# A decode kernel with interleaved layers: query blocks by columns, wider up products, split transposes, output-projection products by shape, and a new planned order

## The chip, the cores and the metric

The kernel runs on one core of a Trainium2 chip. The metric is the device time of one execution in microseconds (us); three runs of the kernel before gave 268.49, 271.14 and 273.38 us, median 271.14. "Faster" or "slower" means by more than 2%.

The core has a matrix engine (PE in the profile, with its weight loads as a row of their own, PEld), a vector engine (DVE), a scalar engine (ACT), a general engine (POOL) and a sync engine (SP), which here issues almost all DMAs. Each engine runs its own list of instructions in order, and they wait for each other through semaphores.

## The reference

Eight rows (batch 8, one query token each, width 448) go through two identical layers of attention over a cached window followed by a small MLP. Both layers use the same weights and, what matters most here, the same K and V.

```
def _A_ref(x, k_cache, v_cache, wq, wo):      # Hq=16, Hkv=8, Dh=256, W=1024 of Sk=4096 kept
    q = (x @ wq).reshape(B, 1, 16, 256)
    k, v = k_cache[:, :, Sk-W:, :], v_cache[:, :, Sk-W:, :]   # each head pair shares one k/v head
    p = softmax(q @ k^T * 256**-0.5)
    return (p @ v).reshape(B, 1, 16*256) @ wo
def _B_ref(x, w1, w2):                         # 448 -> 1792 -> 448
    return silu(x @ w1) @ w2
x = x + _A_ref(_layernorm(x), ...)
x = x + _B_ref(_layernorm(x), ...)
x = x + _A_ref(_layernorm(x), ...)             # the same K, V, wq, wo again
x = x + _B_ref(_layernorm(x), ...)
```

K and V of one row are 16 tiles of 512 KB (8 heads each of K and V, 1024 positions by 256), 128 tiles in all; with the weights the kernel moves 78.31 MB.

## The kernel before

**Staging.** A K or V tile lands in one of 30 slots (`slots`, `load_kv`, L540). The loads stand in a fixed sequence: K of row 0, V of row 0, K of row 1 and so on, with w2 and wo behind the K of row 0 and w1 behind its V. A load waits until the tile that held its slot 30 places earlier has been used for the last time, and that is its use in the second layer. So the K slots of row b come free after the second layer's scores (four after each half, `attend2`), its V slots after the second layer's value products (four after each half, `pv_rows2`, L788).

**Interleaving.** While row b goes through its first MLP and its second attention, row b+1 goes through its first attention, so that every K and V tile is read once from memory and used twice. One turn of this loop ("a row" below) issues some 510 matmuls. In the planned order before it runs like this: `chain(b)` computes the first layer's residual of row b, its statistics (L847, ACT L850, POOL L852), the up products (L587, L592, L598), tanh, the down products (L871), the residual again, the second layer's queries (L882, ACT L887, turned by L890) and stores them as query blocks (L895, eight stores of 32 partitions by 64 numbers); `scores` (L706) is used three times in it, for the next row's first layer in two halves and for this row's second layer in two halves; `softmax` and `pv_rows1`, `pv_cols1` (L756, L770) finish the first layer of row b+1; `wo_rows` (L810) and `wo_cols` (L825, L828) give its output projection, and `pv_rows2` (L788) the second layer's values of row b.

**Shapes on PE.** Scores, value rows, the wide projections and the query products use 32-column tiles of the array, four of them side by side with outputs at partitions 0, 32, 64 and 96. The up products, `pv_cols1`, `wo_cols` and the folds (L571, L574) load full 128-column weights and stream few columns: 28, 32, 16 and 1. The rest of the 448 columns over 3 x 128 gives products of 64 columns (L598, the second L825 form).

**Query blocks.** For each half k2, `qbd` holds 32 blocks of 8 columns beside each other, one block for each of (head j, column block cb, parity par); a block is the weight of one score matmul. Block `a` of 8 columns is loaded as it lies. The second layer's stores L895 write one of every four columns: 64 numbers, each four places from the last.

**Transposes.** A K tile is transposed in place by two DVE instructions (L690), one for each half of the slot. Both write the key `("slot", s)`, so the second waits for the first through DVE's own semaphore.

**The order.** All engine work is recorded as tasks with an estimated duration, the keys that it reads and writes, and a name. A list scheduler (`schedule`) sorts the tasks of each engine by the length of the chain behind them plus a constant out of the table `BIAS`, with `HOLD` deciding how long it holds an engine for a more urgent task. `emit` then writes each engine's list and the waits that the keys ask for. DMAs keep the order of the program. The durations and `BIAS` do nothing on the chip but set this order.

Of the kernel before, what the change touches and what calls it, by code (L numbers as in the profile page):

```python
# [4 lines left out]
BF16 = mybir.dt.bfloat16  # L5
# [14 lines left out]
HOLD = 0.292  # L20
BIAS = {"act.exp0@0": -2.8, "act.exp0@7": -4.3, "act.exp1": 5.0, "act.exp1@0": -4.6, "act.exp1@7": -14.5,
        "act.exp2": 22.7, "act.exp2@0": -145.4, "act.exp2@7": -65.4, "act.init": 4.9, "act.oev0": 15.9,
        "act.oev0@0": 248.8, "act.oev0@7": -0.4, "act.oev1": -97.9, "act.oev1@0": -26.9, "act.oev1@7": 0.1,
        "act.q1s": -9.2, "act.qrow0": 277.6, "act.qrow0@0": 7.0, "act.qrow0@7": -27.8, "act.qrow1": 22.2,
        "act.qrow1@0": -8.1, "act.qrow1@7": -8.4, "act.rowb1": -4.2, "act.rowb1@0": 4.0, "act.rowb1@7": -218.4,
        "act.rowb2": -22.2, "act.rowb2@0": 77.5, "act.rowb2@7": -0.4, "act.rowb8": 12.4, "act.rowb9": 8.5,
        "act.rowbL@7": 75.1, "act.rsum2@0": 50.6, "act.rsum@0": -13.9, "act.tanh": 19.0, "act.tanh8": 171.0,
        "act.tanh@0": 0.7, "act.tanh@7": 20.5, "act.tanhL@7": -81.0, "act.var1": -8.1, "act.var1@0": -10.1,
        "act.var1@7": 63.5, "act.var2": 6.4, "act.var2@0": -0.6, "act.var2@7": 176.2, "act.varL@7": 1.2,
        "act.x2b@7": -13.1, "act.xr@7": 13.6, "act.zL@7": 70.5, "dve.KT0": 88.4, "dve.KT0@0": 228.9,  # L30
        "dve.KT0@7": 27.9, "dve.KT1": 4.3, "dve.KT1@0": 2.0, "dve.KT2": -26.1, "dve.KT2@0": 15.0, "dve.KT3": -88.4,
        "dve.KT3@0": -4.3, "dve.KT3@7": -44.0, "dve.KT4@7": 5.2, "dve.KT5": -900.3, "dve.KT5@0": -16.4,
        "dve.KT5@7": -221.1, "dve.KT6": -10.5, "dve.KT6@0": 4.0, "dve.KT6@7": -151.6, "dve.KT7@7": -27.1,
        "dve.f8a": 1.8, "dve.h8": -3.2, "dve.hT": -24.0, "dve.hTL@7": -48.7, "dve.init": 1.3, "dve.lsum0": 20.2,
        "dve.lsum0@0": -7.1, "dve.lsum1": 3.6, "dve.lsum1@0": 126.7, "dve.lsum1@7": 118.3, "dve.lsum2@0": -1.6,
        "dve.lsum2@7": 18.9, "dve.mT0": -4.0, "dve.mT0@0": 2.9, "dve.mT0@7": 2.7, "dve.mT1@7": 147.6,
        "dve.mT2": 38.0, "dve.mT2@0": -26.3, "dve.mT2@7": -11.8, "dve.max0": -10.8, "dve.max0@0": 37.1,
        "dve.max0@7": 23.9, "dve.max1": -42.3, "dve.max1@0": -12.3, "dve.max1@7": -1.5, "dve.max2": -29.0,
        "dve.max2@0": -2.9, "dve.max2@7": -32.2, "dve.mb0": -84.7, "dve.mb0@0": -0.8, "dve.mb0@7": -81.8,
        "dve.mb1@0": -5.7, "dve.mb1@7": 9.8, "dve.mb2": 2.2, "dve.mb2@0": 20.0, "dve.mg0": -1.5, "dve.mg0@0": 103.5,  # L40
        "dve.mg1": 29.2, "dve.mg1@7": 1.6, "dve.mg2": -0.5, "dve.mg2@0": 17.1, "dve.mg2@7": 3.4, "dve.oTc4": -102.9,
        "dve.oTc4@0": -7.5, "dve.oTc4@7": -1.9, "dve.oTc5@7": -3.1, "dve.oTc6": 0.9, "dve.oTc6@0": -11.3,
        "dve.oTc6@7": 97.4, "dve.oTc7": 1.3, "dve.oTc7@0": -10.2, "dve.oTc7@7": 15.9, "dve.oTev0": -13.1,
        "dve.oTev0@0": 11.1, "dve.oTev0@7": 57.2, "dve.oTev1@7": -0.8, "dve.orow8": 126.6, "dve.orowL@7": 1.9,
        "dve.q1T": 61.4, "dve.q1r": 3.6, "dve.q1s": -17.2, "dve.qbd2.0": 2.2, "dve.qbd2.0@0": -2.6,
        "dve.qbd2.0@7": -63.5, "dve.qbd2.1": -68.8, "dve.qbd2.1@7": -100.3, "dve.rl0": -39.9, "dve.rl0@7": -123.5,
        "dve.rl1@0": 47.5, "dve.rl2": -88.3, "dve.rl2@7": -5.7, "dve.rsum@0": -13.4, "dve.sqh8": 51.5,
        "dve.turn0": -4.9, "dve.turn0@0": 53.7, "dve.turn0@7": 71.5, "dve.turn1": 132.4, "dve.turn1@7": 41.5,
        "dve.turn2": -2.1, "dve.turn2@7": 30.0, "dve.x0": -16.6, "dve.xb0": 29.6, "dve.xb1": 18.8, "dve.xb1@0": 15.5,
        "dve.xb1@7": -1.8, "dve.xb2": 2.7, "dve.xb2@7": -0.7, "dve.xbL@7": -4.6, "dve.xc8": 1.5, "dve.z8": 0.4,  # L50
        "pe.PV0": -1.9, "pe.PV0@0": 54.1, "pe.PV0@7": -368.9, "pe.PV1.0": -461.7, "pe.PV1.0@0": -856.1,
        "pe.PV1.0@7": -57.7, "pe.PV1.1": -22.9, "pe.PV1.1@0": -151.4, "pe.PVc4": 0.3, "pe.PVc4@0": -3.7,
        "pe.PVc4@7": -21.0, "pe.PVc5": -227.6, "pe.PVc5@0": 85.5, "pe.PVc5@7": 6.7, "pe.PVc6": -0.4,
        "pe.PVc6@7": 45.5, "pe.PVc7@0": -3.6, "pe.PVc7@7": -40.3, "pe.S0.0": -28.8, "pe.S0.1": 301.7,
        "pe.S0.1@0": -140.3, "pe.S1.0": -38.9, "pe.S1.0@0": -25.6, "pe.S1.1": 451.9, "pe.S1.1@0": 225.6,
        "pe.S1.1@7": -4.0, "pe.fold1": -35.5, "pe.fold1@0": 4.2, "pe.fold1@7": -1.1, "pe.fold2": 101.9,
        "pe.fold2@7": 7.5, "pe.fold8": 3.7, "pe.fold9": -13.9, "pe.foldL@7": -32.9, "pe.l0": 3.5, "pe.l0@0": -35.3,
        "pe.l0@7": -4.1, "pe.l1": 34.4, "pe.l1@0": 111.0, "pe.l1@7": 0.9, "pe.l2@7": 87.4, "pe.oT0@0": -3.6,
        "pe.oT0@7": -45.7, "pe.oT1": -3.1, "pe.oT1@0": -3.8, "pe.oT1@7": -4.9, "pe.perm0": 1.5, "pe.perm0@0": -9.7,
        "pe.perm0@7": -55.5, "pe.perm1@0": -113.7, "pe.perm1@7": -6.9, "pe.perm2": -21.4, "pe.perm2@0": 17.2,  # L60
        "pe.perm2@7": -17.1, "pe.q1": -6.3, "pe.q1sel": 42.3, "pe.qd0@7": -9.0, "pe.qd1": 110.5, "pe.qd1@0": -0.4,
        "pe.qd1@7": 0.9, "pe.stat1@0": 91.6, "pe.stat1@7": 110.2, "pe.stat2": 4.1, "pe.stat2@0": -17.8,
        "pe.stat2@7": -22.5, "pe.stat8": 0.3, "pe.statL@7": 9.3, "pe.w18": -84.7, "pe.w1@0": -19.9, "pe.w1@7": 3.9,
        "pe.w2": -3.5, "pe.w28": 98.6, "pe.w2@0": 3.8, "pe.w2L@7": -80.2, "pe.wo": -295.7, "pe.wo4": 47.6,
        "pe.wo4@0": -13.7, "pe.wo4@7": 40.3, "pe.wo5@0": 103.1, "pe.wo6": 5.9, "pe.wo6@0": -137.4, "pe.wo6@7": 107.3,
        "pe.wo8": -26.1, "pe.wo@0": 2.1, "pe.wo@7": 1.8, "pe.woL@7": 9.0, "pe.woc@7": 2.5, "pe.wq0": 187.0,
        "pe.wq0@0": 44.9, "pe.wq0@7": 34.9, "pe.wq1": -9.0, "pe.wq1@0": -8.4, "pe.wq1@7": -2.0, "pe.xT": -1.4,
        "pe.xinit": -11.2, "pe.xinit8": 10.3, "pe.xinit@0": 38.4, "pe.xinit@7": -78.5, "pe.xres8": -80.5,
        "pool.init": -0.6, "pool.pow1": -99.7, "pool.pow1@0": -2.2, "pool.pow1@7": 12.4, "pool.pow2@0": -394.4,
        "pool.pow2@7": 21.8, "pool.pow8": 137.9, "pool.powL@7": -1.1, "pool.qbd1": -58.2, "pool.qbd1@0": -181.8,  # L70
        "sp.out": 1.6, "sp.out8": 1.4, "sp.slot0": 5.3, "sp.slot1": 1.6, "sp.slot10": 0.2, "sp.slot11": -3.7,
        "sp.slot12": -0.2, "sp.slot13": -2.2, "sp.slot14": -2.1, "sp.slot15": -2.1, "sp.slot16": -0.1,
        "sp.slot17": -1.0, "sp.slot18": 2.6, "sp.slot19": -4.0, "sp.slot2": -0.5, "sp.slot20": 5.6, "sp.slot21": 0.1,
        "sp.slot22": 3.6, "sp.slot23": 3.4, "sp.slot24": 3.9, "sp.slot25": 2.2, "sp.slot26": -4.1, "sp.slot27": -0.8,
        "sp.slot28": -1.1, "sp.slot29": -4.6, "sp.slot3": -1.4, "sp.slot4": -3.8, "sp.slot5": -5.0, "sp.slot6": 0.6,
        "sp.slot7": -0.1, "sp.slot8": -2.1, "sp.slot9": -2.9, "sp.w1": -1.6, "sp.w1t0": -1.2, "sp.w1t1": -1.2,
        "sp.w2": -0.2, "sp.wo": -1.3, "sp.wq0": 1.2, "sp.wq1": 1.6, "sp.wq2": 1.1, "sp.wqt0": -2.0, "sp.wqt1": -1.8,
        "sp.x": 1.3}
# [230 lines left out]
def bass_interleave_layers__sliding_block_cached__dense_activation_silu__decode_kernel(  # L309
# [23 lines left out]
    C_W1, CW = 96, 28  # L333
# [6 lines left out]
    sb = nc.alloc_sbuf_tensor  # L340
    wq_sb = sb("wq_sb", [P, 3 * HD + HD2], BF16)
    wo_sb = sb("wo_sb", [P, H * PW], BF16)
    w1_sb = sb("w1_sb", [P, 3 * F + F2], BF16)
    w2_sb = sb("w2_sb", [P, FC // 2 * PW], BF16)
    slots = [sb(f"slot{i}", [P, 2048], BF16) for i in range(R)]
    ident = sb("ident", [P, P], BF16)
    perm = sb("perm", [P, P], BF16)
    qbd = [sb(f"qbd{i}", [P, 520], BF16) for i in range(2)]
    ep = [sb(f"ep{i}", [P, 512], BF16) for i in range(2)]
    q1s = sb("q1s", [P, NB, P], BF16)  # L350
    mm = [sb(f"mm{i}", [P, 32], F32) for i in range(2)]
    mg = [sb(f"mg{i}", [P, 8], F32) for i in range(2)]
# [96 lines left out]
    for i in SC:  # L449
        const(bank[i][:], -1e30, bk(i), dur=0.6)  # L450
# [676 lines left out]
```

## Time and profile before

| what | value |
|---|---|
| median of three runs | 271.14 us (268.49 to 273.38) |
| the profiled execution | 271.07 us, span 268.9 us, granted PE clock 0.922 |
| PE, PEld busy | 197.4 us (73%), 130.6 us (49%), 4547 matmuls and as many loads |
| DVE, ACT, POOL busy | 185.3 us (69%), 58.7 us (22%), 23.0 us (9%) |
| DMA | 78.31 MB, mean 291 GB/s |
| L690 transposes | 128, 86.2 us of DVE, 696 ns each |
| L895 query-block stores | 64, 22.5 us of DVE, 352 ns each |
| L706 scores | 1024, 39.8 us of PE |
| L587, L592, L598 up products with 28 columns | 378, 108 and 36 |
| L825, L828 output projection by columns | 160 and 32 |

The span runs from the first to the last instruction of the program; the execution has 2.2 us around it. Matmuls are pipelined, so the times of many add up to more than they take; where it matters, the distance between the starts is used. A busy share is a mean over phases with different limits. The rows "idle before, releaser" tell how long an engine sat idle in front of a group of instructions and what ended that. "issue" means that the engine waited for nothing that the profile records.

### The profile page before, as it was taken

The page shows a single profiled execution, that of the slowest core. Times are in us where ns is not written, and L with a number is a line of the kernel's source. Part 1 is how long each engine was busy: PE and PEld are TensorE (multiplying, and loading weights), DVE is VectorE, ACT ScalarE, POOL GpSimd, SP SyncE. Part 2 cuts the span into 40 slices and gives each one's busy share as a digit, 9 for nine tenths or more (in the row PEclk, how much of TensorE's full clock was granted, in tenths as well). Part 3 has the DMA queues.
Part 4 walks back from the last instruction along what each step waited for, and adds up shares of the span by engine and source line. Part 5 has one row for each costly group of instructions (what it writes and reads, how often), then busy time and mean ns, then how long its engine had stood idle before and what let it go on. Part 6 is the DMA issues. An engine that isn't in the chain of part 4 may idle for free.

```text
span 268.9 us, 10096 instructions
## 1 busy us (share of the span) xinstructions
PE 197.4 (73%) x4547; PEld 130.6 (49%) x4547; DVE 185.3 (69%) x527; ACT 58.7 (22%) x151; POOL 23.0 (9%) x41
## 2 busy tenths in 40 slices
PE   1051333588799788987898879789978897998885
PEld 1051111353567465645565555457455645654644
DVE  6669969767877786688579766986797479313510
ACT  2000537011220320132022102211222032123121
POOL 1200100000010000000000000001001000000200
PEclk9999999999997999599979986998999689979986
DMA  7999999999498999698979969898999697000000
GB/s 194 414 411 390 381 394 410 419 408 406 178 336 306 381 373 388 249 378 268 380 233 396 389 251 333 327 366 309 340 366 376 243 357 278 10 2 2 2 3 0
DMA packets 22639, 78.31 MB, mean 291 GB/s; under 512 B 2231, under 2 KB 5318, under 8 KB 22214
## 3 DMA queue, kind: packets, MB, share of 16 engines
q1 hardware_dynamic: 22438, 77.31, 76.2%
q8 instruction: 35, 0.57, 0.8%
q10 hardware_dynamic: 160, 0.38, 0.6%
q14 instruction: 6, 0.05, 0.0%
HBM read 77.67 MB, written 0.01 MB: 289 GB/s over the span
## 4 chain that ended last, share of the span: by engine, by line
PE 55%; DVE 18%; DMA 10%; issue 5%; ACT 5%; SPq 4%; POOL 1%; DVEq 0%
DMA wo_sb<-in_A_wo_dram 10%; PE bank L788 9%; DVE qbd L895 8%; PE bank L706 8%; PE bank L810 5%; PE bank L587 5%; DVE slot L519 4%; PE bank L770 4%; PE bank L871 4%; PE bank L882 3%; PE bank L825 3%; PE bank L756 3%; ACT ep L835 2%; SPq L540 2%; PE bank L571 2%
## 5 line engine op out<-in xcount | busy, mean ns | idle before, releaser
L690 DVE STREAM_TRANSPOSE slot<-slot 128x512 uint32<-128x512 uint32 x128 | 86.2, 696 | 9.3 <-DMA slot<-in_A_k_cache_dram 8.1
L706 PE MATMUL bank<-slot,qbd 128*8 128x256 bf16 (+1 forms) x1024 | 39.8, 288 | 18.1 <-DVE qbd L895 12.1
L706 PEld LDWEIGHTS bank<-slot,qbd 128*8 128x8 bf16 (+1 forms) x1024 | 22.1, 87 | 29.1 <-DVE qbd L895 18.4
L895 DVE TENSOR_SCALAR qbd<-bank,fcols 32x64 bf16<-32x64 f32 x64 | 22.5, 352 | 7.8 <-PE bank L890 4.2
L788 PE MATMUL bank<-slot,ep 128*2 128x256 bf16 (+1 forms) x512 | 26.4, 359 | 0.0
L729 ACT ACTIVATE ep<-bank,mm 128x256 bf16<-128x256 f32 x24 | 11.4, 473 | 37.5 <-DVE mm L726 24.0
L770 PE MATMUL bank<-qbd,slot 128*128 128x32 bf16 x512 | 17.2, 178 | 3.1 <-DVE q1s L748 2.4
L852 POOL TENSOR_TENSOR fcols<-fcols 128x1 f32<-128x1 f32 x17 | 9.4, 552 | 116.1 <-ACT fcols L850 116.1
L678 POOL TENSOR_TENSOR qbd<-q1s,fcols 128x256 bf16<-128x256 bf16 x16 | 9.8, 612 | 108.2 <-DVE mg L724 37.2
L770 PEld LDWEIGHTS bank<-qbd,slot 128*128 128x128 bf16 x512 | 15.2, 97 | 7.2 <-issue 4.7
L882 PE MATMUL bank<-wq_sb,q1s 128*1 128x512 bf16 x256 | 17.8, 392 | 0.3 <-DVE q1s L840 0.3
L587 PE MATMUL bank<-q1s,w_sb 128*128 128x28 bf16 x378 | 17.9, 184 | 0.0
L840 DVE SCALAR_TENSOR_TENSOR q1s<-bank,fcols 128x5 bf16<-128x5 f32 x17 | 3.9, 230 | 19.2 <-PE bank L828 14.4
L810 PE MATMUL bank<-wo_sb,q1s 128*1 128x449 bf16 x256 | 15.0, 378 | 2.5 <-DVE q1s L775 2.2
L587 PEld LDWEIGHTS bank<-q1s,w_sb 128*128 128x128 bf16 x378 | 14.8, 102 | 2.7 <-DVE slot L690 1.3
L825 PE MATMUL bank<-q1s,wo_sb 128*128 128x16 bf16 (+1 forms) x160 | 11.4, 183 | 6.0 <-issue 6.0
L788 PEld LDWEIGHTS bank<-slot,ep 128*2 128x2 bf16 (+1 forms) x512 | 13.0, 103 | 5.6 <-issue 0.5
L887 ACT ACTIVATE ep<-bank 128x512 bf16<-128x512 f32 x16 | 9.5, 596 | 19.6 <-PE bank L882 18.2
L756 PE MATMUL bank<-slot,qbd 128*2 128x256 bf16 x256 | 9.2, 290 | 6.0 <-DMA slot<-in_A_v_cache_dram 6.0
L592 PE MATMUL bank<-q1s,w_sb 128*128 128x28 bf16 x108 | 13.2, 183 | 0.0
L825 PEld LDWEIGHTS bank<-q1s,wo_sb 128*128 128x128 bf16 (+1 forms) x160 | 8.8, 103 | 7.4 <-issue 6.6
L850 ACT ACTIVATE fcols<-bank,fcols 128x1 f32<-128x1 f32 x17 | 4.4, 259 | 36.0 <-PE bank L847 35.9
(146 smaller groups left out, 281.4 us busy)
## 6 DMA issues: line engine op xcount, KB each, us to landing
slot<-in_A_k_cache_dram SPq DMA_DIRECT2D x64, 512.0 KB, 8.1
slot<-in_A_v_cache_dram SPq DMA_DIRECT2D x64, 512.0 KB, 7.9
wo_sb<-in_A_wo_dram SPq DMA_DIRECT2D x1, 3584.0 KB, 27.3
wq_sb<-in_A_wq_dram SPq DMA_DIRECT2D x3, 1024.0 KB, 8.9
w_sb<-in_B_w_dram SPq DMA_DIRECT2D x1, 1568.0 KB, 19.6
w_sb<-in_B_w_dram SPq DMA_DIRECT2D x1, 1344.0 KB, 17.3
wq_sb<-in_A_wq_dram ACTq DMA_DIRECT2D x1, 256.0 KB, 3.8
wq_sb<-in_A_wq_dram SPq DMA_DIRECT2D x1, 256.0 KB, 4.4
```

What stands on the lines that cost most here:

```text
L587: fns.append(lambda e, f=f, g=g, s=s, c=c, c0=c0: e.matmul(bank[bank_i][:, c0:c0 + cw], w1_sb[:, c * F + 256 * g + s:c * F + 256 * g + s + ...
L592: fns.append(lambda e, t0=t0, c0=c0, g=g: e.matmul(bank[bank_i][:, c0:c0 + cw], w1_sb[:, t0:t0 + 255:2], rhs(3 + (g > 3)), start=False, st ...
L690: dve(lambda e, v=v: e.transpose(v, v), [("slot", s)], [("slot", s)], 0.15 + n / 2 / 950, b, "KT%d" % k)
L706: fns.append(lambda e, w=w, j=j, kv=kv, cb=cb, par=par: e.matmul(sc[32 * j:32 * j + up_to, c0:c0 + 256], w, kv, start=(cb == 0 and par == ...
L729: act(lambda e: e.activation(e_sb[s], x, ACTF.Exp, bias=m[:, 0:1], scale=1.0), bk(sc) + [("mm", L)], E_KEY[s], 0.47, b, "exp%d" % s)
L756: fns = [lambda e, u=u, j=j: e.matmul(bank[OB[0]][32 * j:32 * j + 2, 0:DH], pT_sb[0][:, 32 * u + 10 + 2 * j:32 * u + 12 + 2 * j], slots[sl ...
L770: fns = [lambda e, a=a, u=u: e.matmul(bank[vb][:, c0 + 32 * a:c0 + 32 * a + 32], v[:, u * DH + a:(u + 1) * DH:2], view(pT_sb[1], 32 * u + ...
L788: fns.append(lambda e, u=u, j=j, w=w, k2=k2: e.matmul(bank[OB[1]][32 * j:32 * j + (4, 2)[k2], 0:DH], w, slots[slot_of[b, "v", 4 * k2 + j]] ...
L810: fns.append(lambda e, i=i, w=w, c0=c0: e.matmul(bank[XB][32 * (i % 4):32 * (i % 4) + 1, c0:c0 + D + 1], oT(i), w, start=(i < 4), stop=(i ...
L825: fns.append(lambda e, c=c, rhs=rhs, row=row: e.matmul(bank[YB][xpart(c), XS * c:XS * (c + 1)], xpiece(row, c), rhs.broadcast_to([P, XS]), ...
L882: pe([lambda e, j=j, c=c, wb=wb, k2=k2: e.matmul(bank[wb][32 * j:32 * j + 1, :], xbt[b][:, xcol(c, k2):xcol(c, k2) + 1], wq_sb[:, c * HD + ...
L895: dve(lambda e, qs=qs, k2=k2, q=q: e.tensor_scalar(view(qbd[1][32 * q:32 * q + 32, :], 8 + 256 * k2 + q, [(4, 64)]), qs, rhalf[0:32, :], 2 ...
```

## The change

**Query blocks by columns.** In each half of `qbd` the 8 columns of a block now lie 32 apart: column n of the block index runs fastest. A score matmul loads its 8 (or 16) weight columns with a step of 32. The second layer's stores write two runs of 32 neighbouring numbers in place of 64 scattered ones. The blocks lose their 8 columns of padding; for the second layer's first half, which loads 16 columns, the 8 columns in front are columns of the identity and the permutation matrix, and their results are overwritten by the second half. The queries of the first layer are stored to match (`q_blocks1`, L678).

**Up products.** Each streams 64 columns (the same column repeated) in place of 28, and the 14 results lie 64 apart across two banks that are now one tensor `pair`. Their first matmul starts the bank afresh, so bank XB is written too, and the products now wait for whatever read XB and YB last. The statistics of both kinds sit in YB.

**Value products by columns** stream 64 or 48 columns in place of 32.

**Transposes.** The two halves write keys of their own, so the second no longer waits for the first; `scores` reads all three keys.

**wo column products.** For the last head the 24 products go by shape: 12 of 128 columns, 4 of the mean with 128, 4 of the first 64-column piece, 4 of the second, in place of 3 + 2 + 1 for each of four chunks.

**Order.** All durations and the tables `BIAS` and `HOLD` are new, and with them the order of the tasks on all engines but SP's. In the steady part PE runs the next row's second score half (32 matmuls) before the second layer's first half where it was behind it, turns the second half's queries and does the value rows (L755 in the new numbering) before the second layer's second half, and splits that half around the first value product by columns; the folds of the residual stand behind a score half; 24 of the 32 first value products of the second layer stand behind the wo column products.

```diff
-    C_W1, CW = 96, 28
+    X0, C_ST, CW = 400, 500, 64
...
-    qbd = [sb(f"qbd{i}", [P, 520], BF16) for i in range(2)]
+    cst = sb("cst", [P, 2 * P + 512], BF16)
+    ident, perm = cst[:, 0:P], cst[:, P:2 * P]
+    qbd = [sb("qbd", [P, 512], BF16)[:, :], cst[:, 2 * P:]]
...
+    pair = nc.alloc_psum_tensor("bank6", [P, 1024], F32)[:, :]
+    bank += [pair[:, 0:512], pair[:, 512:1024]]
...
                 for c in range(3):
-                    fns.append(lambda e, f=f, g=g, s=s, c=c, c0=c0: e.matmul(
-                        bank[bank_i][:, c0:c0 + cw], w1_sb[:, c * F + 256 * g + s:c * F + 256 * g + s + 255:2], rhs(c),
-                        start=False, stop=False, skip_group_check=True))
+                    fns.append(lambda e, f=f, g=g, s=s, c=c, out=out: e.matmul(
+                        out, w1_sb[:, c * F + 256 * g + s:c * F + 256 * g + s + 255:2], rhs(c),
+                        start=(f == 0 and c == 0), stop=False, skip_group_check=True))
...
-            dve(lambda e, v=v: e.transpose(v, v), [("slot", s)], [("slot", s)], 0.15 + n / 2 / 950, b, "KT%d" % k)
+            dve(lambda e, v=v: e.transpose(v, v), [("slot", s)], [("kt", s, h)], 0.065 + n / 2 / 950, b, "KT%d" % k)
...
-                    a = 16 + 256 * k2 + (j * 8 + cb * 2 + par) * 8
-                    w = q[:, a - up_to:a]
+                    a = 256 * (k2 if layer else 1 - k2) + j * 8 + cb * 2 + par
+                    w = (cst[:, a:a + 481:32] if up_to == 16 else qbd[layer][:, a:a + 225:32])
...
-        c0 = (256 + 64 * (j // 2), 160)[j % 2]
+        c0, n = ((256, 64), (160, 48), (384, 64), (160, 48))[j]
...
+        for c in list(range(3)) + [XC] + list(range(3, XC)):
+            for i in range(4 * kvh, 4 * kvh + 4):
+                c0 = i // 2 * PW + R0 + i % 2 * D
+                m0 = i // 2 * PW + (M0, M1)[i % 2]
+                w = wo_sb[:, m0:m0 + 1].broadcast_to([P, P]) if c == XC else xpiece(wo_sb[:, c0:c0 + D], c)
+                part, pos = (slice(0, P), (0, 0)) if c == XC else (xpart(c), xpos(c))
...
-        sbk, col = (YB, 490) if name == "2" else (XB, 480)
-        s2 = bank[sbk][:, col:col + 1]
+        s2 = bank[YB][:, C_ST + (name == "2"):C_ST + (name == "2") + 1]
...
-        w1_cols(YB, C_W1, CW, lambda c: xbt[b][:, c:c + 1].broadcast_to([P, CW]), b, [("xbt", b)], "w1", GROUPS)
+        w1_cols(pair, CW, lambda c: xbt[b][:, c:c + 1].broadcast_to([P, CW]), b, [("xbt", b)], bk(XB) + bk(YB), "w1", GROUPS)
...
                 dve(lambda e, qs=qs, k2=k2, q=q: e.tensor_scalar(
-                    view(qbd[1][32 * q:32 * q + 32, :], 8 + 256 * k2 + q, [(4, 64)]), qs, rhalf[0:32, :], 2.0 * SCALE,
-                    op0=ALU.mult, op1=ALU.mult), bk(lb) + ["rhalf"], [("qbd", 1, k2, q)], 0.13, b,
+                    view(qbd[1][32 * q:32 * q + 32, :], 256 * k2 + 32 * q, [(128, 2), (1, 32)]),
+                    qs.rearrange("p (r n) -> p r n", r=2), rhalf[0:32, :], 2.0 * SCALE,
+                    op0=ALU.mult, op1=ALU.mult), bk(lb) + ["rhalf"], [("qbd", 1, k2, q)], 0.14, b,
                     "qbd2.%d" % k2)
```

Left out are the same layout in `q1sel` and in the turn of the second layer's queries (L890), the new column offsets of bank YB, and the tables of the planner.

## The prediction

> **What bounds the kernel now.** I read the page first: the PE clock by slices, the DMA row, and the groups with the longest idle time before them.
>
> ```profile
> PEclk9999999999997999599979986998999689979986
> DMA  7999999999498999698979969898999697000000
> q8 instruction: 35, 0.57, 0.8%
> ...
> L895 DVE TENSOR_SCALAR qbd<-bank,fcols 32x64 bf16<-32x64 f32 x64 | 22.5, 352 | 7.8 <-PE bank L890 4.2
> ```
>
> The reader is to see that the DMA row is full until 62 us (the tenth slice) and has holes once a row afterwards, and that the clock dips at a steady distance. Up to 62 us the weights set the time: wo lands at 39.2 us, four reductions of 2.9 us on DVE follow. After that no engine is full, so the order of time decides. Next, the chain of waits between 112 and 165 us:
>
> ```profile
> 118.47 0.35 DVE qbd L895
> ...
> 119.62 0.36 DVE qbd L895
> 119.98 0.04 issue
> 120.03 1.11 PE bank L706 x26
> ...
> 132.08 1.20 issue
> ...
> 136.77 1.74 PE bank L788 x32
> 138.52 0.78 PE bank L871 x7
> ```
>
> PE stands still for four stores in a row, and again for the four at 121.57; it stands still for 1.2 us inside the wo column products with nothing recorded that it waits for; and 32 matmuls of L788 take 1.74 us. The starts of L871 on this chain (61.01, 87.42, 112.78, 138.52, 164.50, 189.45, 215.37, 239.48 us) give seven rows in 178.5 us, **25.5 us a row**. The view by stages, cut where the clock changes, explains the slow L788:
>
> ```profile
> 131.49:134.91 3.42, 2.22 (x54) 1.73 (x54) 1.35 (x3) 0.00 (x0) 0.00 (x0) 1.00 0.77 307
> 134.91:138.32 3.41, 3.41 (x85) 2.67 (x85) 3.04 (x7) 0.53 (x2) 0.55 (x1) 0.50 0.62 179
> 155.39:158.80 3.41, 1.86 (x42) 1.35 (x38) 1.75 (x4) 0.20 (x1) 0.61 (x1) 1.00 0.92 366
> 158.80:162.21 3.41, 3.41 (x77) 2.60 (x76) 2.62 (x5) 0.26 (x1) 0.55 (x1) 0.50 0.29 74
> ```
>
> The clock (seventh number) changes on a grid of 3.41 us, and each fall to 0.50 follows a stretch with the stall and the narrow products in it; it lasts one or two steps.
>
> **Part by part, for a row.**
>
> *Clock.* I weigh each matmul by its streamed columns, a quarter for 32-column tiles, a half for 64. The groups of PE in 131.49:134.91 (14 x 16, 8 x 16/2, 16 x 256/4 and 16 x 28) give 1,760, and the clock falls; 233.89:237.31 (47 x 28, 16 x 256/4 and less) gives 2,690 and it falls; 90.53:93.95 (24 x 512/4 and 9 x 256/4) gives 3,670 and it stays. So the limit lies between 2,700 and 3,700. A row's 58 up products carry 58 x 28 = 1,624 now and 58 x 64 = 3,712 then. With the stall and only 16 up products in the stretch it would be 2,340, still too little; without the stall all fit in, 4,500 and more. So this gain hangs on the stall. Its price: the second half of L788 takes 1.81 us where the 32 like-shaped matmuls of L756 take 0.97 at full clock, 0.84 every row; in every second row (two steps) L871 takes 0.65 and the first half of L788 0.41 more, so 0.53 on average: 1.37. Wide products cost 64 columns at 107 ns per 256 (four tiles of L706 side by side), 27 ns in place of 25: 58 x 2 = 0.1. **-1.3**; at half clock they would cost 53 ns, +1.5.
>
> The Trainium skill (TensorE: Matmul & The Clock Gate, section "HAM oscillation") says that PE idle for more than about 3 us is what brings the clock down. The longest idle time of a row here is 1.55 us, and it falls every row. By the page the wide columns would return nothing, and the row below would be 1.3 us longer.
>
> *Stall.* It comes 1,024 PE instructions apart (510 matmuls, as many loads, some waits), at 81.73, 106.10, 132.08, 157.12, 183.69 and 208.25 us: 0.56, 0.94, 1.20, 1.55, 0.45, 1.30, none in the last row, mean 0.86. 35 packets of 16 KB for 9,150 PE instructions make 256 each, four a row; one runs from 131.0 to 132.0 us, 1.3 us before PE goes on. So PE waits for code. Counting 256 back, that packet could be asked for at 126.6 us; L540 had eight loads issued around then, and the packet came behind some 5.5 pending tiles of 1.28 us (512 KB at 410 GB/s). With under one tile pending the packets of other blocks start after 0.5 to 1.7 us. After the change the block edges fall on the same counts: again near the end of the column products, but the edge before moves into the second layer's second score half, ahead of the four loads that this half releases. I expect some 2 to 3 tiles pending there, 3 us + 1.0 + 1.3 against a block that takes 5.5. I leave 0.3: **-0.55**; bounds -0.86 and +1.
>
> The skill (Runtime: NRT & Kernel Launch, section "Instruction fetch mechanics") calls the crossing of a 16 KiB block mostly hidden. The rows above show up to 1.55 us; by the page this term would be nothing.
>
> *Stores.* L895 writes 64 scattered bf16 in 352 ns. Two rows show the price of scatter:
>
> ```profile
> L656 DVE TENSOR_TENSOR slot<-slot 128x256 bf16<-128x256 f32 x1 | 1.3, 1269 | 0.0
> L669 DVE CAST q1s<-bank 128x512 bf16<-128x512 f32 x1 | 0.7, 655 | 0.0
> ```
>
> L656 stores with a step, L669 in a run: 5.0 against 1.3 ns a number. L866 (14 numbers) takes 167 ns and L737 (64 read, 8 written) 222, so I take 205 for the new store, bounds 167 and 352. Eight stores a row save 8 x 0.147 = 1.2 on the path, and the order puts the next row's score half (1.07) before the first wait (0.93 idle) and the turn and the value rows (1.4) before the second (0.66). Both go: **-1.3** of 1.6. If the stores stay at 352, that cover still takes about 0.6.
>
> *Column products.* L825 to a 64-column form costs 99 ns and back 129, other starts are 25 to 39 apart: 0.33 for each of four chunks, 1.33. By shape: 24 x 25 and one change, 0.7. All on the path: **-0.6**.
>
> *Order.* The 0.5 at 126 us, where PE waits for the turn (L733) of probabilities, gets a quarter of the scores beside it: **-0.4**, bounds 0 and -0.7.
>
> *Transposes.*
>
> ```profile
> 130.57 1.45 DVE L690 STREAM_TRANSPOSE slot<-slot 128x512 uint32<-128x512 uint32 x2
> 137.28 1.30 DVE L690 STREAM_TRANSPOSE slot<-slot 128x512 uint32<-128x512 uint32 x2
> ```
>
> A pair with the wait takes 1.45, two of different tiles 1.30; 0.11 to 0.15 for most of eight pairs, 0.8 of DVE. Scores rarely wait for L690, so **0** on PE's path; it is what lets the second score half come early.
>
> *Waits and costs added.* The up products now wait for ACT's read of the statistics (0.26 and the way there); 16 matmuls of L788 (0.54) lie between, so 0; without them +0.4 with all of PE's list behind. Weight columns with a step of 32: no row has them. L890 streams the identity with that step at 27 ns a start, and step-2 weights load in 102 ns against 97; if a column cost the 3.3 ns that a scattered store does, 8 x 3.3 x 128 = 3.4 us a row unhidden. I take 0, since loads lie beside the stream; nothing makes it a gain. Value products at 64 or 48: 64 x 1.7 ns = 0.1, inside the rounding.
>
> Sum: 1.3 + 0.55 + 1.3 + 0.6 + 0.4 = 4.15, a row of 21.35. **Two floors are near:** 16 tiles x 1.28 = 20.5 us of DMA, and the four fetches, 5 us each, 20. Where three limits are so near they cost each other something: I add 0.65 and forecast **22.0 us a row**, 7 x 3.5 = 24.5. The last row saves 1.2 with its stores and some clock, 1.5 in all; up to 62 us nothing (wide products at the half clock that holds there cost 1.5, and the clock rises sooner). 271.07 - 26 = **245 us**, against a median of 271.14, so no correction.
>
> **Rivals.**
> *Stall and clock stay* (0.19): the fuller DMA queue holds the code back at another edge, the clock still falls, and the wide products run partly at 53 ns. Left are 1.3 + 0.6 + 0.4 less some 0.8: 1.5 a row, 259 us, from 251 to 265. For it: latency follows the pending tiles, and a denser row has more. Against it: the edge moves ahead of four loads.
> *Stores stay at 352 ns* (0.05): the layout does not do what it says; about 0.8 a row less, 251 us.
> *Within 2%* (0.07): the first rival with weight loads partly unhidden, 267 us.
> *Slower* (0.05): code becomes the bound. From request to first instruction it took 126.6 to 133.3, 6.7 us, behind 5.5 tiles. If the packed row put all four of its fetches there, a row would be 26.8, 280 us. It decides from 6.4 us a fetch on; the shortest blocks now have 3 to 4.
> *As forecast* (0.64): 236 to 252.
>
> **Numbers.** Below 236 would need a row at the floor of 20.5 us (0.03, with the forecast). The range **236 to 262** leaves out the upper end of the first rival, the last two, and that corner: under 2 in 10. A measurement tells 2% (5.4 us) from no change. Faster 0.88, within 2% 0.07, slower 0.05.
>
> **What the changed profile would show.** L890 in the new numbering (the stores) near 205 ns; the clock row at 9 from 62 to 250 us; "issue" inside L825 under 0.5 us or gone; L787 with 32 matmuls in about 1 us in every row; L866 starts 22 us apart; the DMA row without holes. It would be wrong if the clock still dips once a row, if "issue" shows at L704 or L866, or if DVE waits for K tiles.

## The result and the profile after

The changed kernel takes 259.37 us (median of four runs, 256.68 to 262.17), the kernel before 271.28 us beside it: a ratio of 0.951, with an interval from 0.937 to 0.966. The medians count all runs, a ratio and its interval only those within 1.5% of the fastest of their kernel. The forecast was 245, so the kernel is faster but by half of what was expected. 259 us is the time that the first rival, "stall and clock stay", gave. The profiled run took 262.17 us, the longest of the four, with a span of 258.5 (before: a span of 268.9).

The page of the kernel after: the granted clock and the DMA row by slices, the code queue, and the groups that answer to those of before (line, engine, operation, then busy time and mean ns of one, then idle time before them and what ended it).

```profile
PEclk9999999999999999799979988999999799999995
DMA  6999999999669989996999699879979995200000
q8 instruction: 35, 0.57, 0.9%
...
L689 DVE STREAM_TRANSPOSE slot<-slot 128x512 uint32<-128x512 uint32 x128 | 80.3, 678 | 4.5 <-DMA slot<-in_A_k_cache_dram 4.5
...
L890 DVE TENSOR_SCALAR cst<-bank,fcols 32x64 bf16<-32x64 f32 x64 | 17.3, 270 | 6.3 <-PE bank L885 4.2
L787 PE MATMUL bank<-slot,ep 128*2 128x256 bf16 (+1 forms) x512 | 20.8, 291 | 0.1
```

A store (L890) takes 270 ns, not 205. The clock still falls, now in four rows, for one step each. The DMA row still has its holes. The chain of waits shows where a row goes (start, length in us, what):

```profile
110.45 0.79 PE bank L866 x13
...
126.91 0.63 PE bank L825 x21
127.54 0.81 issue
128.35 0.26 PE bank L825 x3
128.61 0.91 PE bank L787 x24
129.51 0.20 PE bank L842 x4
129.71 0.95 PE bank L787 x9
...
130.99 0.16 PE bank L589 x3
...
134.90 0.79 PE bank L866 x12
```

The idle time without a cause ("the stall" below) inside L825 is there as before, in every row of the loop that has loads running: 0.28 us at 80.7, then 0.63, 0.81, 0.55, 1.21 and 1.67 us at 103.3, 127.5, 152.2, 176.4 and 200.7 us. Behind four of these six the clock is at one half: the view by stages, one line ahead of the fall and one behind it (PE, weight loads, DVE, ACT, POOL, then clock, DMA share, GB/s):

```profile
125.66:129.08 3.42, 2.61 (x76) 2.09 (x78) 2.21 (x7) 0.54 (x1) 0.61 (x1) 1.00 0.96 367
129.08:132.49 3.41, 3.41 (x64) 2.30 (x52) 2.78 (x5) 0.26 (x1) 0.55 (x1) 0.50 1.03 387
```

The length of the stall does not decide it: behind the 0.55 us at 152.2 the clock falls too, and behind the 1.21 us at 176.4 it stays up. From the chain, then the view by stages:

```profile
176.43 1.21 issue
```

```profile
176.86:180.27 3.41, 2.63 (x75) 2.04 (x75) 2.30 (x5) 0.26 (x1) 0.55 (x1) 1.00 1.01 411
```

The starts of L866 on the chain, 110.45, 134.90, 159.40, 182.95, 208.91 and 231.06 us, make five rows in 120.6 us, **24.1 us a row**. The forecast was 22.0, the row before 25.5.

### The profile page after: what moved, and what is told of

Same layout as the page of the kernel before. It is cut to its first block, busy times and chain, and to the rows that moved or that the text cites. A ratio compares the mean times of both kernels' runs of the same rounds, so it can differ in the third digit from the quotient of the medians.

```text
span 258.5 us, 10100 instructions
## 1 busy us (share of the span) xinstructions
PE 197.5 (76%) x4547; PEld 133.5 (52%) x4547; DVE 179.1 (69%) x526; ACT 57.5 (22%) x151; POOL 23.0 (9%) x41
## 4 chain that ended last, share of the span: by engine, by line
PE 51%; DVE 22%; DMA 16%; issue 4%; SPq 4%; ACT 2%; DVEq 0%; ACTq 0%
DMA wo_sb<-in_A_wo_dram 11%; PE bank L704 9%; DVE slot L689 8%; PE bank L589 8%; PE bank L787 7%; PE bank L809 5%; DMA slot<-in_A_v_cache_dram 5%; DVE cst L890 5%; PE bank L769 5%; DVE slot L521 4%; PE bank L825 3%; SPq L542 2%; PE bank L866 2%; PE bank L594 2%; PE bank L885 1%
## 5 line engine op out<-in xcount | busy, mean ns | idle before, releaser
L689 DVE STREAM_TRANSPOSE slot<-slot 128x512 uint32<-128x512 uint32 x128 | 80.3, 678 | 4.5 <-DMA slot<-in_A_k_cache_dram 4.5
L704 PE MATMUL bank<-slot,qbd 128*8 128x256 bf16 x512 | 21.3, 304 | 6.6 <-ACT ep L728 4.0
L589 PE MATMUL bank<-q1s,w_sb 128*128 128x64 bf16 x378 | 24.3, 215 | 0.5 <-ACT fcols L845 0.5
L589 PEld LDWEIGHTS bank<-q1s,w_sb 128*128 128x128 bf16 x378 | 20.7, 112 | 3.9 <-ACT fcols L845 2.1
L704 PE MATMUL bank<-slot,cst 128*8 128x256 bf16 (+1 forms) x512 | 19.5, 282 | 3.1 <-DVE cst L890 2.6
L890 DVE TENSOR_SCALAR cst<-bank,fcols 32x64 bf16<-32x64 f32 x64 | 17.3, 270 | 6.3 <-PE bank L885 4.2
L769 PEld LDWEIGHTS bank<-qbd,slot 128*128 128x128 bf16 x512 | 16.8, 101 | 7.1 <-issue 4.8
L704 PEld LDWEIGHTS bank<-slot,qbd 128*8 128x8 bf16 x512 | 14.7, 97 | 10.9 <-DVE mm L725 4.5
L769 PE MATMUL bank<-qbd,slot 128*128 128x48 bf16 (+1 forms) x512 | 19.6, 193 | 0.8 <-DVE q1s L774 0.5
L809 PE MATMUL bank<-wo_sb,q1s 128*1 128x449 bf16 x256 | 17.8, 376 | 1.9 <-DVE q1s L774 1.6
L678 POOL TENSOR_TENSOR qbd<-q1s,fcols 128x256 bf16<-128x256 bf16 x16 | 9.8, 613 | 104.1 <-DVE cst L890 29.4
L594 PE MATMUL bank<-q1s,w_sb 128*128 128x64 bf16 x108 | 18.6, 214 | 0.0
L704 PEld LDWEIGHTS bank<-slot,cst 128*8 128x8 bf16 (+1 forms) x512 | 12.3, 101 | 7.8 <-DVE cst L890 7.0
L755 PE MATMUL bank<-slot,qbd 128*2 128x256 bf16 x256 | 10.6, 289 | 6.7 <-DMA slot<-in_A_v_cache_dram 6.7
L720 DVE TENSOR_REDUCE mm<-bank 128x1 f32<-128x256 f32 x24 | 10.1, 423 | 4.5 <-PE bank L704 3.8
L521 DVE TENSOR_REDUCE slot<-wo_sb 128x6 f32<-128x2688 bf16 x4 | 11.8, 2945 | 1.0 <-DMA wo_sb<-in_A_wo_dram 1.0
```

What stands on the lines that cost most here:

```text
L521: dve(lambda e, rows=rows, s=s: e.tensor_reduce(s, rows[:, :, R0:M1].rearrange("p c (a n) -> p c a n", a=2), AX.X, ALU.add, negate=True), ...
L589: fns.append(lambda e, f=f, g=g, s=s, c=c, out=out: e.matmul(out, w1_sb[:, c * F + 256 * g + s:c * F + 256 * g + s + 255:2], rhs(c), start ...
L594: fns.append(lambda e, t0=t0, out=out, g=g: e.matmul(out, w1_sb[:, t0:t0 + 255:2], rhs(3 + (g > 3)), start=False, stop=True, skip_group_ch ...
L689: dve(lambda e, v=v: e.transpose(v, v), [("slot", s)], [("kt", s, h)], 0.065 + n / 2 / 950, b, "KT%d" % k)
L704: fns.append(lambda e, w=w, j=j, kv=kv, cb=cb, par=par: e.matmul(sc[32 * j:32 * j + up_to, c0:c0 + 256], w, kv, start=(cb == 0 and par == ...
L755: fns = [lambda e, u=u, j=j: e.matmul(bank[OB[0]][32 * j:32 * j + 2, 0:DH], pT_sb[0][:, 32 * u + 10 + 2 * j:32 * u + 12 + 2 * j], slots[sl ...
```

## Experiments

Four parts were taken back one at a time, with the order of every engine left as it is after the change; then the order was exchanged; then the code edges were moved; then the loads were made lighter. Each ratio is to runs of the kernel before beside it (272.6 to 272.9 us). For two kernels, chunks and oldorder, the comparison gives no interval, so their medians and extremes stand.

**Width of the up products (narrow).**

```diff
-    X0, C_ST, CW = 400, 500, 64
+    X0, C_ST, CW = 400, 500, 28
```

> Only the width of the up products goes back, from 64 streamed columns to 28; the order of every engine and all else stays as after the change. Theory A (the forecast's clock term): the stretch of 3.41 us around the up products loses 58 x 36 = 2,088 weighted columns, the clock stays at one half for a second step in most rows and falls in rows where it now stays up (173, 197); mean granted clock near 0.92 as before the change, and 0.8 to 1.3 us a row more, 265 to 268 us. Rival B: the wide products return nothing, because the stall still brings the fall and a wide product costs 53 ns at half clock; mean clock within 0.01 of 0.961, time within 2 us of 259.

Measured: 257.46 us (256.23 to 263.68), 0.945 [0.939, 0.950], mean clock 0.956 in the profiled run. For the time that is rival B, for the clock it is not: over the six runs the mean clock is 0.905 to 0.956, against 0.941 to 0.979 in the four runs after the change, and a run with 0.930 took 256.23 us. The page's clock row, and a row of the chain in which the stall is small:

```profile
PEclk9999999999999799999967999999599999999995
```

```profile
151.44 0.63 PE bank L825 x20
152.07 0.35 issue
152.42 0.27 PE bank L825 x4
...
154.36 0.07 PE bank L589 x3
...
156.07 0.57 PE bank L787 x16
```

With products of 28 columns and 0.35 us of stall the clock stays up: three products in 0.07 us. In the row before this one, with a stall of 1.45 us (126.67), it falls, and for two steps where the kernel after has one. So in the new order a row can keep the clock without the wide products, and with them it can lose it; they seem to shorten the fall, but no time hangs on that.

**wo column products by chunks (chunks).**

```diff
-        for c in list(range(3)) + [XC] + list(range(3, XC)):
-            for i in range(4 * kvh, 4 * kvh + 4):
...
+        for i in range(4 * kvh, 4 * kvh + 4):
...
+            for c in range(XC):
...
```

> Only the wo column products go back to the order by chunks, six products of one chunk after the other with four changes of tile shape. Theory A (the forecast's term): L825's products take 1.3 us a row in place of 0.9 and all of it is on PE's path, 0.4 to 0.6 us a row, 262 to 264 us. Rival B: PE waits for DVE or for code later in the row anyway, the lost time is taken back there; the products take 1.3 us but the time stays within 1.5 us of 259.

Measured: 262.56 us (257.64 to 264.52); 3.2 more than after, inside theory A's bounds. In a row without a stall its 24 products take 1.35 us until the next group starts (127.67 to 129.02); by shape, in light below, they take 0.64. So the price of the chunks is there. That the time follows is not shown: the two sets of runs overlap, and their fastest are 257.64 and 256.68 us.

**Layout of the query blocks (scatter).**

```diff
-                    view(qbd[1][32 * q:32 * q + 32, :], 256 * k2 + 32 * q, [(128, 2), (1, 32)]),
-                    qs.rearrange("p (r n) -> p r n", r=2), rhalf[0:32, :], 2.0 * SCALE,
+                    view(qbd[1][32 * q:32 * q + 32, :], 8 + 256 * k2 + q, [(4, 64)]), qs, rhalf[0:32, :], 2.0 * SCALE,
...
-                    w = (cst[:, a:a + 481:32] if up_to == 16 else qbd[layer][:, a:a + 225:32])
+                    w = qbd[layer][:, a - up_to:a]
```

> Only the layout of the query blocks goes back: stores scattered four numbers apart, score weights in a run; order as after the change. Theory A: a store takes 350 ns again in place of 270, eight a row on the path, 0.65 us a row, 263 to 265 us (with the 205 ns that the forecast took it would be 268). Rival B: weight columns with a step of 32 cost the score products what the stores save; then the score loads and products of L704 get shorter by 0.3 us a row or more and the time stays within 2 us of 259.

Measured: 258.94 us (255.66 to 263.45), 0.947 [0.941, 0.953]. The groups of this kernel by lines (L891 is the store, L826 the column products):

```profile
L705 PE MATMUL bank<-slot,qbd 128*8 128x256 bf16 (+1 forms) x1024 | 39.3, 285 | 15.2 <-DVE qbd L891 7.9 <-ACT ep L729 4.0 <-DVE slot L690 3.2
L891 DVE TENSOR_SCALAR qbd<-bank,fcols 32x64 bf16<-32x64 f32 x64 | 22.3, 349 | 6.2 <-PE bank L886 4.2
L826 PE MATMUL bank<-q1s,wo_sb 128*128 128x16 bf16 (+1 forms) x192 | 7.6, 173 | 3.0 <-issue 3.0
```

The store takes 349 ns again and PE waits 7.9 us for stores, where after the change it waits 2.6. Theory A had the mechanism right, yet the time does not rise. Rival B has little for it: loads of score weights take 87 ns here and 97 to 101 ns with the step of 32, and a score product 285 against 293 ns on average, which for 128 a row in four tiles side by side is 0.26 us a row at most, and the clock of this run is the higher one. What went down is the stall: 3.0 us inside the column products, against 5.1 after the change. **Here the row with more waiting in it has less stall.** One profile each shows this, of runs of 255.66 and 262.17 us, and no run below varies the waiting alone, so it is a reading and not shown.

**Waits between the halves of a K tile's transpose (pairs).** The edit adds, once the order is fixed, a dependency of each second half on the first.

> Only the second half of each K tile's transpose waits for the first half again, 0.11 to 0.15 us for each of 8 pairs a row. Theory A (the forecast): this is DVE time beside PE's path, the time stays within 1 us of 259. Rival B: the chain of waits after the change runs through L689 (8% of the span) between the softmax steps, so of the 0.9 to 1.2 us a row that the waits cost DVE some half are on the path, 262 to 266 us.

Measured: 259.3 us (256.84 to 260.38), 0.951 [0.945, 0.956]. L689 is busy for 85.6 us in place of 80.3, and the time is that of after: the forecast's 0 holds.

**The order alone, and all else alone (neworder, oldorder).** Both kernels get their engines' order as a written list.

```diff
     pl.schedule()
+    for e in ORDER:
+        own = [t for t in pl.tasks if t.eng == e]
+        pl.order[e] = [own[int(i)] for i in ORDER[e]]
```

> The kernel before with one thing changed: every engine's instructions come in the order of the kernel after; layouts, widths, column products by chunks and the waits of the transposes stay as they were. Theory A (order is what brought the gain, since taking back width, layout or waits one by one moved the time by under 0.7%): 258 to 264 us, PE no longer waits for four stores in a row without other work. Rival B (the forecast's sum: the order is worth 0.4 and the cover of the stores 0.6 us a row): 264 to 266 us. Rival C (the parts carry it together, each hides the others): 269 us or more.

> The kernel after with every engine's instructions in the order of before (only the first group of up products stays behind the statistics); layouts, widths, column products by shape and independent transposes stay. Theory A (order brought the gain): 268 us or more, the waits for four stores with nothing beside them come back. Rival B (the forecast: stores 0.66 as measured, clock 1.3, column products 0.6 us a row do not need the order): 256 to 262 us. Rival C (the parts carry it together and the order nothing): 259 us.

Measured: the kernel before in the new order 262.76 us (258.61 to 265.00), 0.959 [0.949, 0.969]; the kernel after in the old order 273.45 us (265.88 to 277.54), against 272.85 before: theory A of both. **By the medians the order brings 10 us without the parts, and the parts bring nothing without the order.** What the parts add to the new order (259.37 against 262.76 us) is not clear of noise: the two intervals overlap. The lines of before, then of oldorder, then of neworder:

```profile
L706 PE MATMUL bank<-slot,qbd 128*8 128x256 bf16 (+1 forms) x1024 | 39.8, 288 | 18.1 <-DVE qbd L895 12.1 <-POOL qbd L678 6.0
L825 PE MATMUL bank<-q1s,wo_sb 128*128 128x16 bf16 (+1 forms) x160 | 11.4, 183 | 6.0 <-issue 6.0
```

```profile
L635 PE MATMUL bank<-q1s,w_sb 128*128 128x64 bf16 x378 | 28.5, 233 | 3.2 <-ACT fcols L891 3.2
L750 PE MATMUL bank<-slot,cst 128*8 128x256 bf16 (+1 forms) x512 | 18.4, 281 | 7.2 <-DVE cst L936 7.1
L871 PE MATMUL bank<-q1s,wo_sb 128*128 128x16 bf16 (+1 forms) x192 | 7.5, 177 | 8.7 <-issue 8.3
```

```profile
L752 PE MATMUL bank<-slot,qbd 128*8 128x256 bf16 (+1 forms) x1024 | 40.7, 293 | 18.0 <-DVE qbd L941 8.0
L871 PE MATMUL bank<-q1s,wo_sb 128*128 128x16 bf16 (+1 forms) x160 | 11.2, 182 | 1.6 <-issue 1.5
```

In the old order the faster stores do cut PE's waits for them from 12.1 to 7.1 us. Then, in this profile (of a run of 277.54 us, four above the median), 2.3 us come back as stall (6.0 to 8.3), 3.2 us as the new wait of the up products for the statistics (0.4 a row, what the forecast named for the case that no L788 lies between), and the up products stand in the half clock more often (233 ns each, 215 after the change). In the new order the waits for stores fall to 8.0 us and the stall inside the column products to 1.5: the order moves the code edges against the bursts of loads as well. How much of its 10 us is the one and how much the other, these two runs can't tell.

**Moving the code edges (pad112, pad64, pad76, bpad112).** Products of one column that add nothing to the result are put ahead of all others on PE, in its idle time at the start. Each is two instructions with its load.

```diff
+    pe([lambda e: e.matmul(bank[LB[0]][:, 0:1], ident, ident[:, 0:1], start=True, stop=True)
+        for _ in range(112)], ["ident"], bk(LB[0]), 0.0, -1, "spare")
     load_tails()
```

> The kernel after with 112 products of one column of the identity ahead of everything on PE (224 instructions with their loads, done while PE waits for the first weights); they add nothing to the result. All later instructions stand 224 places further, so the edges of 256 fall 32 instructions later in a row. Theory A (PE waits for code, and the block of the column products is left in 5.1 us, too short for its fetch): by after's own trace the block that holds them now lasts 5.9 us, the idle time without a cause inside L825 is gone or under 0.3 us, and some shows up after L866 instead, where 4 to 5 tiles are pending; with the stall the half clock goes in most rows, rows of 23.0 to 23.8 us, 252 to 256 us in all. Rival B (the idle time belongs to the place, not to the count): it stays inside L825 with 0.5 to 1.7 us, 259 us.

> The kernel after with 64 such products (128 instructions) ahead of everything: the edges fall in the middle between those of after, behind the value products of L787 and inside the score halves. Theory A (code): the idle time leaves L825 and comes back where a block is short and tiles are pending, by after's trace at the second layer's scores (blocks of 5.0 and 5.6 us): the time is not lower than after's, 258 to 266 us. Rival B (the idle time belongs to the place): it stays inside L825, 259 us. Rival C (any shift helps): 252 to 256 us.

> The kernel after with 76 products of one column ahead of everything on PE, code edges 104 instructions later. By the traces of after and of the run with 112 products no block with pending tiles is then shorter than its packet's way by more than 0.2 us. Theory A (places of the edges): at most 0.3 us of idle time without a cause a row, 252 to 256 us. Rival B (the row needs four fetches of 5.5 to 6 us whatever the place, so what goes at one edge comes at another): 256 to 262 us; with 128 instructions it was 267.

> The kernel before with 112 products of one column ahead of everything on PE, so that its code edges fall 32 instructions later. By its own trace the block that holds the column products then lasts 6.0 to 6.6 us, more than the packet's way. Theory A (the stall is a matter of where the edges fall, and the clock follows it): 0.9 us of stall and half of 1.4 us of clock a row go, 260 to 266 us. Rival B (a denser row makes the stall again 32 instructions later, as in the kernel after): 268 to 273 us.

Measured, with the kernel after 0.951: 112 products 256.06 us (254.21 to 259.98), 0.943 [0.935, 0.951]; 64 products 267.02 us, 0.983 [0.976, 0.991], not lower than after, as theory A had it, and 1 us above its range; 76 products 263.59 us, 0.974 [0.966, 0.983], above both of its theories. The kernel before with 112: 266.79 us, 0.987 [0.977, 0.998], just above theory A's range. The chain of the kernel with 112 products, then with 76:

```profile
125.34 0.64 PE bank L825 x24
125.98 0.53 PE bank L787 x13
126.51 0.73 issue
127.24 0.50 PE bank L787 x11
```

```profile
132.00 0.20 PE bank L589 x3
132.22 0.03 PE bank L589
132.26 1.34 issue
133.59 0.22 PE bank L589 x2
```

After the change the stall stands behind the 21st of L825's 24 products. With 224 instructions more (256 - 32) it stands 3 + 13 = 16 products further on, which are the 32 instructions, and with 152 more (256 - 104) it stands 52 products further on. It goes by the count of instructions modulo 256, whatever the line: rival B of the first two runs falls. All runs of this case say the same: counting PE's instructions (loads and waits too) in the order of their starts from 0, the 75 stalls of over 0.25 us that 13 of the 14 kernels have between 62 and 250 us (light, below, has none) all stand at 193 or 194 modulo 256, and in each PE goes on 1.2 to 1.6 us after a packet of code has landed. But theory A's "gone" falls too. With 112 products 0.43 to 1.33 us a row remain at the new place, though after's trace had given that block 5.9 us; up to the stall it now takes 5.3 to 5.5 us, and its packet starts 3.6 to 4.2 us after the edge. That the half clock had made it long before, and that a denser row runs into the edge again, fits these numbers but is not shown apart. Two of the three places are worse than the one that the kernel happened to have: with 76 products the stalls stand in L589 and in the value products of L769, with 64 in L809 and in L589, 10 to 12 us in these lines, not at the scores where the expectation put them. The version with 112 products has the lowest median of all that do the whole computation; its interval overlaps that of after. For the kernel before the same shift is worth 5.8 us: inside L825 the stall is gone, one of 0.74 us and smaller ones remain in L788 (2.3 us in all), and the clock falls all the same.

**Lighter loads (light, blight).**

```diff
+        nu = 4 if s in first_use else 8
         first_use.add(s)
-        dma(lambda e: e.dma_start(slots[s][:, :].rearrange("p (u d) -> p u d", d=DH),
-                                  cache[b, kvh, S0:SK, :].rearrange("(p u) d -> p u d", p=P)),
+        dma(lambda e: e.dma_start(slots[s][:, 0:nu * DH].rearrange("p (u d) -> p u d", d=DH),
+                                  cache[b, kvh, S0:SK, :].rearrange("(p u) d -> p u d", p=P)[:, 0:nu, :]),
```

> The kernel after, but from the 31st K or V tile on only half of each tile is loaded (256 KB in place of 512); the other half keeps what lay there, so from row 1 on the scores and values are not those of the reference. All engines do the same instructions. Theory A (PE waits for code because the packet lies behind pending tiles): packets start within 2 us of the edge, the idle time inside L825 is gone, and with it the half clock in the rows; rows of 22.3 to 23.0 us, 246 to 251 us. Rival B (the idle time has nothing to do with the loads): 0.5 to 1.7 us stay inside L825, 256 us or more. Rival C (the forecast's row of 22.0 us is there once nothing is held back): 245 us or less.

> The kernel before with the same halved loads from the 31st tile on (the other half of a tile is not loaded, so scores and values are not those of the reference). It tells whether the order's gain is one of PE's and DVE's waits or of the places where the code edges fall. Theory A (waits for the stores, the turn and the changes of shape): the stall goes here too, but the row stays 1.0 to 1.5 us longer than in the kernel after with the same loads, 256 to 261 us. Rival B (the order's gain was that of fewer held-back fetches and the clock): within 3 us of the kernel after with the same loads.

These two kernels leave out half of each later tile, so their results are not the reference's. Measured: after with half the bytes 249.26 us (248.11 to 249.61), 0.921 [0.913, 0.928], inside theory A's bounds; before with half the bytes 267.05 us, 0.989 [0.979, 0.999]. The page of light, its groups, and its chain:

```profile
PEclk9999999998899999999999999999999999999795
DMA  6999999999938554782876377377828742000000
...
L690 DVE STREAM_TRANSPOSE slot<-slot 128x512 uint32<-128x512 uint32 x128 | 80.0, 676 | 4.6 <-DMA slot<-in_A_k_cache_dram 4.6
...
L756 PE MATMUL bank<-slot,qbd 128*2 128x256 bf16 x256 | 10.6, 289 | 7.4 <-DMA slot<-in_A_v_cache_dram 7.4
```

```profile
107.88 0.79 PE bank L867 x12
...
124.27 0.64 PE bank L826 x24
124.91 0.76 PE bank L788 x24
...
126.62 0.09 PE bank L590 x3
...
129.93 0.28 PE bank L867
```

No stall, full clock from 63 to 230 us, and five rows of L867 (L866 after the change) from 107.88 to 218.14 us: **22.05 us a row, the forecast's 22.0.** The waits for K and V tiles in these lines (4.6 and 7.4 us against 4.5 and 6.7) all lie in the first 62 us, where the tiles are still whole. Later the weight loads of L769 wait 1.6 us for V tiles in the kernel after, PE itself 0.2, and in light nothing does, so data that came sooner is a small part. What changed is the code's way: its packet starts 1.6 to 2.6 us after the edge ahead of the column products, where after the change it took 3.5 to 4.7 us.

Where the time went is seen row by row. The five rows of light are 10.35 us shorter than those of after. From L866 to the start of L825 the five rows differ by 1.1 us; the other 9.2 lie behind the first column product. From there to the next L866 it takes 7.99, 7.88, 7.15, 8.84 and 4.96 us after the change, and 5.66, 5.66, 5.67, 5.66 and 4.96 in light: the fifth row, where the loads have come to their end, is the same in both. Less the stall (0.81, 0.55, 1.21, 1.67 us), the three rows in which the clock fell lose 1.5 to 1.7 us more, and the one in which it stayed up 0.3. The halved loads also halve the floor that the DMA sets, so this run does not say that the whole kernel could reach 22 us a row.

In blight the stall is at most 0.17 us in the rows from 114.60 on, but the clock still falls once a row:

```profile
PEclk9999999999999799769988997999799799979886
...
L789 PE MATMUL bank<-slot,ep 128*2 128x256 bf16 (+1 forms) x512 | 25.7, 353 | 0.0
```

Its rows last 24.2 us (114.60 to 235.55 in five). With half the bytes the change is worth 17.8 us (267.05 - 249.26, 2.1 a row); with all of them, 12. Theory A of blight, 1.0 to 1.5 us a row and 256 to 261 us, had the sign and was too small. What of the 17.8 is order and what the parts, no run with half the bytes tells.

## Why the prediction was right and wrong

The sign, the range and the view of what bounds the kernel hold: no engine is full, the order of time decides. The case that was given 0.64 did not come, and by the prediction's own signs (the clock dips, "issue" shows at L866) its mechanism failed. The rival with 0.19 came in what it said would be seen: stall and clock stay. That it has the microsecond is luck. Its sum counts the stores, with their cover by the order, at 1.3 and the order at 0.4, where the runs showed 0.65 and more than 0.4, and its reason is not what the trace shows: the stall stands at the same edge as before, and not behind a fuller queue.

*The stall is the step that failed.* "I expect some 2 to 3 tiles pending there, 3 us + 1.0 + 1.3 against a block that takes 5.5. I leave 0.3." The tiles and the block were about right: at the edge ahead of each of the five stalls from 103.3 us on 2.7 to 3.0 tiles were issued and not yet landed, and from there to the stall it took 5.3 to 5.6 us. The wait for the packet was mis-sized: it started 3.5 to 4.7 us after the edge, took 0.9 to 1.0, and PE went on 1.3 to 1.6 us after it. Fewer tiles did not bring it sooner: in the kernel before, with 3.5 to 5.6 pending, it started after 3.6 to 4.5 us. So over seven rows the stall is 0.74 us a row (5.1 in all) against 0.86 before, 0.12 saved for 0.55.

The stall was treated as a cost that a better place lowers. The runs fit better with a limit: each block of 256 PE instructions needs the way of its packet, and what is saved between two edges is waited for at the second. That would explain why taking back the layout or the width costs nothing; it is argued, not shown. The forecast's second floor, four fetches of some 5 us a row, was too low in any case: the stalled blocks took 5.9 to 7.2 us from edge to edge, and the missing 2 us a row went there and into the clock behind it.

*The clock's gain came only in part.* Three falls of 1.5 to 1.7 us in five rows are some 0.9 us a row, against 1.37 before, so some 0.4 of the 1.3 came (an estimate from these rows). The prediction hung it on the stall. With the stall gone (light) the clock does stay up; but it also stayed up behind 1.21 us of stall, and in blight, in the old order, it falls without one. The upper bound of the limit, 3,700 weighted columns, was misread: eight of the 24 wide products counted in 90.53:93.95 had started before that stretch, and counted by starts it carries some 2,600 and keeps the clock. Counted so, in all 14 kernels from 64 to 238 us, the clock fell behind stretches with 961 to 3,079 and was kept by stretches with 2,580 and more. Four stretches of after ahead of a fall carry 2,439 to 2,890, the two of narrow behind a stall 1,862 and 2,599: the wide products add to a stretch, but where a stall lies in it that is mostly not enough.

*Stores:* mis-sized, 270 ns for 205, 0.65 us a row for 1.2. The 205 came from rows that write 14 and 8 numbers; 64 numbers in two runs cost more than either.

*Order:* its -0.4 and the cover of 0.6 for the stores were 1.0 us a row; alone it measured 10 us in all, 1.4 a row, of which a part is stall and clock.

*Column products by shape:* 24 in 0.64 us, 0.7 forecast; taken back they cost 3.2 us by the medians, 0.45 a row for 0.6, inside the spread.

*Transposes, strided weights, added waits at 0:* hold in the new order (pairs; loads of 97 to 101 ns for 87, beside the stream). In the old order the wait for the statistics cost the 0.4 named.

*The sum:* 22.0 us a row is what light shows, without the DMA's floor near it. There the stores' missing 0.5 us and the 0.3 left for the stall about cancel, which is luck.

Of the skill's two rules the prediction set the trace first, and rightly. "Runtime: NRT & Kernel Launch", section "Instruction fetch mechanics", calls the crossing of a block mostly hidden: with light tiles in the queue it is, with full ones PE stands still for up to 2.4 us at a time. "TensorE: Matmul & The Clock Gate", section "HAM oscillation", gives the rule of no idle gaps over some 3.4 us: the clock fell here behind 0.55 us of unexplained idle time, and in blight behind 0.17.

## What to carry to other kernels

Here idle time without a cause that returned at the same count modulo 256 was code that came late, and it came late with tiles pending in the DMA queue: count the instructions between two stalls first. Then expect that a saving ahead of it may be waited for at the next edge, and do not simply subtract the stall; a run with half the bytes shows what the rest of a change is worth without it. Padding ahead of the loop moved the time from 256 to 267 us, so two versions that differ in a few instructions can differ by that alone.

## What the runs showed of the hardware

- The place of the stall follows the instruction count: 16 products further for 224 more instructions, 52 for 152; all 75 stalls of these runs stand at 193 or 194 modulo 256.
- Halving the bytes of the loads took every stall of over 0.25 us away behind 62 us in the kernel after, and four of six in the kernel before.
- The packet of code started 3.5 to 4.7 us after its edge with 2.7 to 3.0 tiles of 512 KB pending, and 3.6 to 4.5 with 3.5 to 5.6.
- The granted clock fell to one half behind stretches with at most 0.17 us of unexplained idle time, where the work was thin (2,138 to 2,626 weighted columns in the step before).
- A store of 64 numbers takes 349 ns scattered by four and 270 in two runs of 32; weight loads of eight columns take 97 to 101 ns with a step of 32 and 87 in a run.
- 64 waits between two transposes on the same engine cost DVE 5.3 us, 83 ns each (85.6 against 80.3 us).
